# Opening of an attention and mixture-of-experts kernel: shift rows sent by SyncE, router constants made earlier or by ScalarE, one pair's copies held back

## The chip, the cores and the metric

The kernel runs on one core of a Trainium2 chip. Its engines are named as in the profile: PE is TensorE (PEld its weight loads), DVE is VectorE, ACT is ScalarE, POOL is GpSimd, SP is SyncE, which here only issues DMAs. A row marked SPq or ACTq is the issue of a DMA by that engine's sequencer. The metric is the device time of one execution in microseconds (us), as the median over runs.

## What is computed

Causal attention with a forgetting bias over 8 batches, 8 heads, 576 positions and head size 64, and then a two-level mixture of 16 experts on the 4608 resulting tokens. Cut to what matters:

```python
scores = q @ k.T / 8
cum = cumsum(maximum(s, 0))                    # per head
scores += minimum(-(cum[:, None] - cum[None, :]), 0);  scores[causal] = -1e9
attn = exp(scores - max(scores)) ;  x = (attn / sum(attn)) @ v
group = argmax(x @ w_group) ;  expert = argmax(x @ w_expert[group])
out = weight * (maximum(x @ w1[expert], 0) @ w2[expert])
```

## The kernel before, in words

Heads are handled in 32 pairs; pair p holds heads 2p and 2p+1. The loop `for step in range(-LEAD, NH + 5)` does at step n the scores and exponentials of head n, the product with the values of head n-1, and the row maxima of head n+4. The order of the work within a step is written out by hand in lists of letters (`FIRST`, `ORDERS`), so that the order on PE, DVE, ACT and POOL is fixed. Steps -4 to -1 do only the row maxima of the first four heads.

The operands of the scores stand in tiles that are used in turn. `WA` (four of them, `NA`) holds keys and queries rounded to fp32r, and below them the rows with the running sums (two) and the row shifts (two). `WB` (five, `NBB`) holds the low parts of the same. For each pair:

- `load_raw` (L159, SP) brings keys and queries, 576 KB, into a tile `r`; there are three.
- `split` (L166 on ACT, L170 on POOL, for the first pair on DVE) rounds them into `hl` and takes the low part. For the first four pairs `place` (L182, ACT) writes half of `WA` and `WB` directly.
- `load_a` (L191, L193, SP) copies `hl` and the sums into `WA`, and `load_b` (L203, L204, SP) copies `hl` into `WB`, from the fifth pair on in four copies of 144, 288, 144 and 288 KB. `load_v` (L207, SP) brings the values `VT`.
- `rowmax` (L228 on PE, L236 on DVE) gives the row maxima. When a pair has all of them, they are transposed (L250) and `shifts` (L256, L257 on DVE) makes their negative in two parts, `th` and `tl`, of 10 partitions by 128. `send` (L262) then issues two DMAs that write them as two rows of `WA`. In the kernel before, these DMAs are issued by ACT: 64 in all.
- `scores` (L284 and L286 on PE) needs these rows. It writes into a ring of three PSUM tiles `ps`, which come free when the exponential (L294, ACT) has read them. A head has five such units. `av` (L326) multiplies with the values into `po`, which come free when ACT has copied `vals` and `sums` (L331, L334).

Each DMA issued by SP or ACT ends on one of eight semaphores that are given out in turn over both queues (DMAHW0 to DMAHW7 in the listings below). The issue of a DMA waits until the DMA that used its semaphore before has landed. The issue also waits for the data it reads and for the place it writes. An engine's queue is in order, so whatever stands behind such an issue waits too.

The sums: `s` arrives, DVE scales and scans it (L530, L532), rounds it (L533) and subtracts (L534), and SP copies the two parts into the first `WA`. The router's constants (`ub`, `ob`, and through `ni` the two tables `part`) are made by DVE in `operands`, in between the row maxima of the third and fourth head.

## Time and profile before

| | us |
|---|---|
| three runs | 867.61, 872.62, 871.92; median 871.92 |
| the profiled execution | 869.25 |
| its span, first to last instruction | 867.4 |
| PE busy | 839.2 (97%) |
| DVE, ACT, POOL busy | 718.4, 615.0, 602.5 |

The attention takes somewhat less than the first half of the span; the experts follow. The page's 40 slices show PE at 90% or more busy in all but the first, the third and the last. A row of the timeline gives the start, the duration, the engine, the line, what is written from what, and in brackets the idle time of the engine ahead of it with what ended it. In a row of windows stand the window, its length, the busy time of each engine with the number of instructions, the granted clock of PE as a share of 2.4 GHz, the share of time the DMA engines were busy, and GB/s.

### The profile page before, as it was taken

How to read it: one execution, taken by the hardware profiler on the slowest of the kernel's cores; microseconds unless marked ns; L12 is line 12 of the kernel's file. 1: busy time of each engine (PE TensorE's matmuls, PEld its weight loads, DVE VectorE, ACT ScalarE, POOL GpSimd, SP SyncE). 2: the span in 40 equal slices, each digit the busy share in tenths (PEclk: the TensorE clock that was granted, in tenths of full speed). 3: DMA queues.
4: the chain of work that ended last, by engine and by line, in shares of the span. 5: the costliest groups of instructions: out<-in, count | busy, mean ns of one | idle time of the engine just before them, and what ended most of it. 6: DMA issues, size and time to landing. Idle time of an engine off the chain costs nothing. (4 is left out here: it accounts for less than half of the span.)

```text
span 867.4 us, 17805 instructions
## 1 busy us (share of the span) xinstructions
PE 839.2 (97%) x5601; PEld 771.9 (89%) x5601; DVE 718.4 (83%) x1982; ACT 615.0 (71%) x1393; POOL 602.5 (69%) x745
## 2 busy tenths in 40 slices
PE   4989999999999999999999999999999999999997
PEld 2778888888888888887789999999999999999996
DVE  7657788797878889787859799989999999999972
ACT  5668778786878778777747666776677777778760
POOL 9767677676876769545867756776677777777760
PEclk9999999999999999999999999999999999999999
DMA  7899898897979888633646645655566565666620
GB/s 197 266 233 250 234 235 232 213 248 194 248 209 245 236 221 225 177 87 122 194 149 225 245 151 208 205 164 193 201 201 216 188 216 195 223 228 214 215 96 26
DMA packets 82405, 174.06 MB, mean 201 GB/s; under 512 B 9692, under 2 KB 45660, under 8 KB 74112
## 3 DMA queue, kind: packets, MB, share of 16 engines
q1 hardware_dynamic: 72192, 153.20, 60.2%
q0 software_dynamic: 7488, 18.89, 5.7%
q10 hardware_dynamic: 2624, 0.76, 0.4%
q8 instruction: 46, 0.75, 0.3%
q14 instruction: 55, 0.45, 0.2%
HBM read 108.97 MB, written 19.69 MB: 148 GB/s over the span
## 5 line engine op out<-in xcount | busy, mean ns | idle before, releaser
L1067 POOL TENSOR_TENSOR wl<-raw,wh 128x512 fp32r<-128x512 f32 x163 | 209.8, 1299 | 82.5 <-ACT wh L1064 54.6
L236 DVE CUSTOM_DVE_ANT_0 mx<-pm,mask 128x192 bf16<-128x192 f32 (+4 forms) x320 | 127.3, 418 | 33.1 <-PE pm L228 30.4
L1064 ACT CAST wh<-raw 128x512 fp32r<-128x512 f32 x256 | 154.3, 616 | 0.0
L1189 PE MATMUL ph<-xh,wh 128*128 128x256 f32 (+13 forms) x512 | 140.2, 300 | 0.1
L1189 PE MATMUL ph<-xl,wh 128*128 128x256 f32 (+13 forms) x512 | 137.7, 300 | 0.1
L228 PE MATMUL pm<-WA 66*128 66x288 f32 (+4 forms) x384 | 123.8, 355 | 14.0 <-DMA WA<-ch 9.7
L284 PE MATMUL ps<-WA 68*128 68x320 f32 (+4 forms) x384 | 135.4, 356 | 1.7 <-DMA WA<-tl 1.6
L326 PE MATMUL po<-pt,VT 128*128 128x256 f32 (+3 forms) x512 | 119.0, 351 | 3.6 <-POOL pt L303 1.8
L1196 ACT ACTIVATE hh<-ph 128x256 fp32r<-128x256 f32 (+13 forms) x128 | 53.5, 418 | 85.5 <-PE ph L1189 83.3
L1269 PE MATMUL py<-hh,wh 128*128 128x256 f32 (+13 forms) x448 | 113.4, 302 | 0.1
L1269 PE MATMUL py<-hl,wh 128*128 128x256 f32 (+13 forms) x448 | 112.5, 301 | 0.0
L286 PE MATMUL ps<-WB 128*128 128x320 f32 (+4 forms) x384 | 110.2, 300 | 0.0
L1322 DVE STREAM_TRANSPOSE yr<-yT 32x384 f32<-32x384 f32 (+1 forms) x208 | 104.6, 503 | 4.5 <-ACT yT L1266 0.3
L326 PE MATMUL po<-pu,VT 128*128 128x320 f32 (+1 forms) x384 | 105.2, 382 | 0.0
L1159 DVE STREAM_TRANSPOSE xt<-xg 32x256 f32<-32x256 f32 (+1 forms) x208 | 102.3, 492 | 2.7
L326 PEld LDWEIGHTS po<-pt,VT 128*128 128x128 f32 x512 | 87.8, 191 | 16.6 <-POOL pt L303 2.5
L1189 PEld LDWEIGHTS ph<-xh,wh 128*128 128x128 f32 x512 | 95.3, 189 | 0.6 <-DVE hl L1197 0.3
L1189 PEld LDWEIGHTS ph<-xl,wh 128*128 128x128 f32 x512 | 94.7, 189 | 0.5 <-DVE xl L1142 0.3
L1189 PE MATMUL ph<-xh,wl 128*128 128x256 f32 (+13 forms) x512 | 91.9, 299 | 0.0
L170 POOL TENSOR_TENSOR WB<-r,hl 64x576 fp32r<-64x576 f32 x62 | 88.0, 1420 | 5.5 <-ACT hl L166 1.7
L228 PEld LDWEIGHTS pm<-WA 66*128 66x128 f32 (+1 forms) x384 | 68.9, 192 | 24.0 <-POOL WA L528 9.6
L422 POOL TENSOR_TENSOR xTl<-xT,xTh 128x512 fp32r<-128x512 f32 x29 | 37.0, 1275 | 75.9 <-ACT xTh L417 55.7
(255 smaller groups left out, 2001.0 us busy)
## 6 DMA issues: line engine op xcount, KB each, us to landing
raw<-in_w_dram SPq DMA_DIRECT2D x64, 1024.0 KB
r<-in_qk_dram SPq DMA_DIRECT2D x32, 576.0 KB
WA<-hl SPq DMA_DIRECT2D x60, 288.0 KB
WB<-hl SPq DMA_DIRECT2D x60, 288.0 KB
VT<-in_v_dram SPq DMA_DIRECT2D x32, 384.0 KB
WB<-hl SPq DMA_DIRECT2D x64, 144.0 KB
xs<-xr SPq DMA_DIRECT2D x15, 512.0 KB
WA<-cumd SPq DMA_DIRECT2D x56, 4.5 KB
```

What stands on the lines that cost most here:

```text
L170: (nc.vector if p < 1 else nc.gpsimd).tensor_tensor(out=hl[:, 2] if part else WB[p % NBB][0:64, KA, h], in0=r[hr, part], in1=hl[hr, part]. ...
L228: nc.tensor.matmul(ps[:rows, :cw], WA[i][0:66, QA, h, QO + q0:QO + q0 + rows], WA[i][0:66, KA, h, QO + c0:QO + c0 + cw], start=True, stop= ...
L236: nc.vector.tensor_tensor_reduce(out=tmp[:rows, :cw], in0=ps[:rows, :cw], in1=mk[:rows], scale=1.0, scalar=-3.0e38 if c0 == 0 else mo, op0 ...
L284: nc.tensor.matmul(ps[:rows, o:o + w], WA[i][0:68, KA, h, QO + k0:QO + k0 + rows], WA[i][0:68, QA, h, QO + q0:QO + q0 + w], start=True, st ...
L286: nc.tensor.matmul(ps[:rows, o:o + w], WB[p % NBB][:, KA, h, k0:k0 + rows], WB[p % NBB][:, QA, h, q0:q0 + w], start=False, stop=True)
L326: nc.tensor.matmul(po[0][:, qa - base:qb - base], VT[p % NVT].rearrange("p t a d -> p (t a d)")[:, (3 * t + 1 + h) * 64:][:, 0:P], x[:, c: ...
L1064: self.casts.append(nc.scalar.copy(h[:, j], raw[:, j]))
L1067: self.low = lows[self.u, i, j] = nc.gpsimd.tensor_tensor(out=l[:, j], in0=raw[:, j], in1=h[:, j].bitcast(F32), op=ALU.subtract)
L1159: V.transpose(dst[:, 0:n, :, j], src[:, 0:n, :, i])
L1189: self.product = nc.tensor.matmul(pss[f][:, :cap], w[f // 4][:, c, (f % 4) * P:(f % 4 + 1) * P], x[:, c, :cap], start=(c == 0 and w is sel ...
L1269: self.product = nc.tensor.matmul(pss[c][:, :cap], w[2 + f // 4][:, f % 4, c * P:(c + 1) * P], x[:, f, :cap], start=(f == 0 and w is self. ...
L1322: V.transpose(dst[:, 0:n, :, i], src[:, 0:n, :, j])
```

## The change

Four things are changed, all of them in the attention part.

1. `send` issues the DMAs of `th` and `tl` on SP's queue, for all 32 pairs.
2. The rounding of the sums (was L533) goes from DVE to ACT, and at the start `place(0, 0)` is put behind the first pair's `split`.
3. The router's constants: the four operations that make `part` stand ahead of the sums on DVE; `ub` and `ob` are written by ACT at the end of step -1; only the rounding of the router's weights stays among the row maxima, later than before.
4. The four `load_b` copies of the sixth pair (p = 5) are held until the last exponential of head 4, and behind the last `load_a` copy of their pair.

```diff
-                nc.sync.dma_start(w[64:66, KA, h, QO:].bitcast(F32), (cumh if p < 4 else cumd)[n:n + 1].bitcast(F32))
+                st.at["wa", p] = nc.sync.dma_start(w[64:66, KA, h, QO:].bitcast(F32), (cumh if p < 4 else cumd)[n:n + 1].bitcast(F32))
...
-                if h or not placed:
-                    nc.sync.dma_start(w[0:64, QA, h], hl[hr, 1])
-                nc.sync.dma_start(w[64:128, b, h], hl[hr, 0::2][:, b])
+                copies = [nc.sync.dma_start(w[0:64, QA, h], hl[hr, 1])] if h or not placed else []
+                copies.append(nc.sync.dma_start(w[64:128, b, h], hl[hr, 0::2][:, b]))
+                for i in copies if p == 5 else ():
+                    hold(tc, i, st.at["exp", 4])
+                    behind(tc, i, st.at["wa", p])
...
-                    nc.scalar.dma_start(WA[i][r:r + 1, QA].bitcast(F32).rearrange("o h q -> o (h q)"), t.bitcast(F32))
+                    nc.sync.dma_start(WA[i][r:r + 1, QA].bitcast(F32).rearrange("o h q -> o (h q)"), t.bitcast(F32))
...
+        nc.gpsimd.iota(n1, pattern=[[S, B], [P, NB]], base=1, channel_multiplier=1, allow_small_or_imprecise_dtypes=True)
+        for k, x, op in ((0, 6, ALU.arith_shift_right), (1, 63, ALU.bitwise_and)):
+            nc.vector.tensor_scalar(out=ni, in0=n1, scalar1=x, scalar2=None, op0=op)
+            nc.vector.tensor_copy(part[:, k], ni)
         nc.vector.tensor_scalar(out=r1, in0=s0, scalar1=0.0, scalar2=8.0, op0=ALU.max, op1=ALU.mult)
...
-        nc.vector.tensor_copy(cumh[:, 0], c2)
+        nc.scalar.copy(cumh[:, 0], c2)
...
-        place(0, 0)
         split(0, 0)
         split(0, 1)
+        place(0, 0)
         load_a(0, True)
...
                 nc.sync.dma_start(cumd, cumh.bitcast(F32))
+                nc.scalar.copy(rt.ub, rt.uf)
+                nc.scalar.copy(rt.ob, rt.onesf)
                 rt.queue.append(rt.operands())
...
-        yield 5
+        yield 11
         V.tensor_copy(self.wr_sb[:, :, 0:20], self.wr_f)
         V.tensor_tensor(out=self.wr_sb[:, :, 20:40], in0=self.wr_f, in1=self.wr_sb[:, :, 0:20].bitcast(F32),
                         op=ALU.subtract)
-        yield
-        V.tensor_copy(self.ub, self.uf)
-        yield
-        V.tensor_copy(self.ob, self.onesf)
-        yield
-        V.tensor_scalar(out=ni, in0=n1, scalar1=6, scalar2=None, op0=ALU.arith_shift_right)
-        V.tensor_copy(self.part[:, 0], ni)
-        yield
-        V.tensor_scalar(out=ni, in0=n1, scalar1=63, scalar2=None, op0=ALU.bitwise_and)
-        V.tensor_copy(self.part[:, 1], ni)
```

The order of PE's matmuls does not change in any row. What moves is seen in three places.

The first is SP's queue at the start, which in the kernel before reads as follows. `WA_107` and `WB_111` belong to the first pair, `WA_108` and `WB_112` to the second, `WA_109` with `r_135` and `hl_223` to the third; `r_346` holds the raw data of the fourth pair and `VT_116` the first values.

```order
L204 DMA WB_111<-hl_171 64x576
L193 DMA WA_109<-ch 2x1x576
L191 DMA WA_109<-hl_223 64x2x576
L193 DMA WA_109<-ch 2x1x576
L204 DMA WB_112<-hl_180 64x2x576
L203 DMA WB_112<-hl_180 64x576
L204 DMA WB_112<-hl_180 64x576
L207 DMA VT_116<-in_v_dram 128x6x128
L159 DMA r_346<-in_qk_dram 128x1152
```

In the changed kernel the same place of SP's queue reads as follows, with what each issue waits for; `hl_227` is the third pair's rounded data and `r_350` the fourth pair's raw data.

```order
L203 DMA WB_111<-hl_178 64x576 [waits DMAHW5_49]
L202 DMA WB_113<-hl_227 64x576 [waits DMAHW6_49,Activation_49]
L264 DMA WA_107<-th_293 1x10x128 [waits DMAHW7_49,DVE_49]
L264 DMA WA_107<-tl_294 1x10x128 [waits DMAHW0_49,DVE_49]
L193 DMA WA_109<-ch 2x1x576 [waits DMAHW1_49,Pool_49]
L191 DMA WA_109<-hl_227 64x2x576 [waits DMAHW2_49]
L193 DMA WA_109<-ch 2x1x576 [waits DMAHW3_49]
L203 DMA WB_112<-hl_188 64x2x576 [waits DMAHW4_49,Pool_49]
L202 DMA WB_112<-hl_188 64x576 [waits DMAHW5_49]
L203 DMA WB_112<-hl_188 64x576 [waits DMAHW6_49]
L209 DMA VT_116<-in_v_dram 128x6x128 [waits DMAHW7_49]
L159 DMA r_350<-in_qk_dram 128x1152 [waits DMAHW0_49]
```

Three issues have come in ahead of the third pair's first row of sums: a copy of the third pair's data, which waits for ACT, and the first pair's two shift rows. The raw data of the fourth pair are now the tenth issue behind the copy that waits for ACT.

The second place is ACT's queue at the fourth and fifth step of the loop (heads 4 and 5), before the change, with the waits. `th_711` and `tl_712` are the shift rows of the fourth pair.

```order
L294 ACTIVATE pt_118<-ps_2_0_692 128x512 [waits Pool_49]
L262 DMA WA_110<-th_711 1x10x128 [waits DMAHW4_49,DVE_49]
L262 DMA WA_110<-tl_712 1x10x128 [waits DMAHW6_49,DVE_49]
L334 ACTIVATE sums_596<-po_0_686 64x256
L294 ACTIVATE pu_119<-ps_0_256_702 128x320 [waits PE_49]
L294 ACTIVATE pt_118<-ps_4_0_719 64x64 [waits PE_49]
```

The two issues are gone from ACT's queue in the changed kernel:

```order
L296 ACTIVATE pt_118<-ps_2_0_692 128x512 [waits Pool_49]
L336 ACTIVATE sums_594<-po_0_686 64x256
L296 ACTIVATE pu_119<-ps_0_256_702 128x320 [waits PE_49]
L296 ACTIVATE pt_118<-ps_4_0_719 64x64 [waits PE_49]
L166 CAST hl_673<-r_591 128x576
```

The third place is SP's queue at the same time. Before, semaphore DMAHW6, for which the issue of `tl_712` above waits, was last used by the first copy into `WB_111`, which is the sixth pair's (`hl_580`).

```order
L207 DMA VT_116<-in_v_dram 128x6x128 [waits DMAHW4_49,PE_49]
L159 DMA r_743<-in_qk_dram 128x1152 [waits DMAHW5_49]
L203 DMA WB_111<-hl_580 64x576 [waits DMAHW6_49]
L191 DMA WA_108<-hl_580 64x2x576 [waits DMAHW7_49,PE_49]
L193 DMA WA_108<-cumd 2x576 [waits DMAHW0_49]
L204 DMA WB_111<-hl_580 64x2x576 [waits DMAHW1_49,Pool_49]
L203 DMA WB_111<-hl_580 64x576 [waits DMAHW2_49]
L204 DMA WB_111<-hl_580 64x2x576 [waits DMAHW3_49]
L159 DMA r_915<-in_qk_dram 128x1152 [waits DMAHW5_49]
```

In the changed kernel the four copies stand behind the next raw load and the shift rows, and the first of them waits for ACT; `hl_578` is the sixth pair's.

```order
L159 DMA r_743<-in_qk_dram 128x1152 [waits DMAHW5_49]
L191 DMA WA_108<-hl_578 64x2x576 [waits DMAHW6_49,PE_49]
L193 DMA WA_108<-cumd 2x576 [waits DMAHW7_49]
L159 DMA r_915<-in_qk_dram 128x1152 [waits DMAHW0_49,Pool_49]
L264 DMA WA_110<-th_711 1x10x128 [waits DMAHW1_49,DVE_49]
L264 DMA WA_110<-tl_712 1x10x128 [waits DMAHW2_49,DVE_49]
L193 DMA WA_109<-cumd 2x576 [waits DMAHW3_49,PE_49]
L202 DMA WB_111<-hl_578 64x576 [waits DMAHW4_49,Activation_49]
L191 DMA WA_109<-hl_673 64x2x576 [waits DMAHW5_49,Activation_49]
L203 DMA WB_111<-hl_578 64x2x576 [waits DMAHW6_49]
```

From there on, SP's queue has for nearly every pair the raw load, then `th` and `tl`, then the row of sums.

## Rows read from the trace of the kernel before

**Rows 1.** The page's first part: busy time, share and instructions of each engine.

```profile
PE 839.2 (97%) x5601; PEld 771.9 (89%) x5601; DVE 718.4 (83%) x1982; ACT 615.0 (71%) x1393; POOL 602.5 (69%) x745
```

**Rows 2.** Windows: three pairs of steps, and the stretch behind a stall.

```profile
34.43:47.86 13.43, 11.89 (x68) 9.21 (x66) 12.29 (x38) 9.97 (x23) 10.99 (x15) 1.00 0.91 240
47.86:62.38 14.52, 12.72 (x72) 11.09 (x70) 7.95 (x30) 9.36 (x23) 7.75 (x11) 0.88 0.94 232
62.38:73.30 10.92, 10.92 (x72) 9.75 (x70) 7.98 (x30) 8.77 (x24) 7.40 (x12) 1.00 0.89 229
55.30:58.70 3.40, 3.35 (x12) 3.08 (x13) 1.00 (x5) 2.76 (x7) 0.23 (x1) 0.50 0.86 250
```

**Rows 3.** Timeline, 44 to 55 us: the fourth pair's shift rows and SP's raw loads.

```profile
44.78 1.33 SPq L159 DMA_DIRECT2D r<-in_qk_dram  x1
...
50.44 0.28 DVE L257 SCALAR_TENSOR_TENSOR tl<-pmt,th 10x128 fp32r<-10x128 f32 x1
...
53.79 0.36 SPq L159 DMA_DIRECT2D r<-in_qk_dram  x1
54.10 0.73 ACTq L262 DMA_DIRECT2D WA<-tl  x1
...
54.87 0.38 ACT L334 ACTIVATE sums<-po 64x256 f32<-64x256 f32 x1 [3.53 <-DVE mc L236]
```

**Rows 4.** Timeline, 36 to 44 us: router constants on DVE, and ACT's exponential.

```profile
36.58 1.43 DVE L749 CAST ub<-uf 128x128 bf16<-128x128 f32 x1
...
40.26 0.54 ACT L294 ACTIVATE pu<-ps 128x448 f32<-128x448 f32 x1 [1.65 <-DVE mc L236]
...
43.42 0.18 DVE L757 CAST part<-ni 128x40 f32<-128x40 int32 x1
```

**Rows 5.** Timeline, 0 to 23 us: loads, casts and the first shift rows.

```profile
1.46 1.51 SPq L159 DMA_DIRECT2D r<-in_qk_dram  x3
...
4.17 0.50 DVE L530 TENSOR_SCALAR cl<-cl 64x576 f32<-64x576 f32 x1 [4.17 <-DMA cl<-in_s_dram]
...
5.65 1.15 ACT L182 CAST WA<-r 64x1152 fp32r<-64x1152 f32 x1 [3.03 <-DMA r<-in_qk_dram]
...
6.08 0.74 DVE L533 CAST ch<-cl 64x576 fp32r<-64x576 f32 x1
...
13.87 1.24 ACT L166 CAST hl<-r 128x576 fp32r<-128x576 f32 x2
...
18.07 0.74 ACTq L262 DMA_DIRECT2D WA<-tl  x1
...
18.67 0.61 SPq L207 DMA_DIRECT2D VT<-in_v_dram  x1
...
19.33 1.15 SPq L159 DMA_DIRECT2D r<-in_qk_dram  x2
...
22.21 0.55 PE L284 MATMUL ps<-WA 68*128 68x256 f32 x1 [1.57 <-DMA WA<-tl]
```

**Rows 6.** Timeline, 24 to 33 us: casts of the fourth pair, and PE's pace.

```profile
24.35 0.57 PE L286 MATMUL ps<-WB 128*128 128x448 f32 x1
...
26.81 1.15 ACT L182 CAST WA<-r 64x1152 fp32r<-64x1152 f32 x1
...
30.38 0.48 ACT L294 ACTIVATE pt<-ps 64x64 f32<-64x64 f32 x2
...
31.83 0.37 PE L286 MATMUL ps<-WB 128*128 128x448 f32 x1
...
32.19 0.31 PE L284 MATMUL ps<-WA 68*128 68x320 f32 x1
```

**Rows 7.** Timeline, 222 to 231 us: shift rows of a later pair, and its first scores.

```profile
222.23 0.75 SPq L159 DMA_DIRECT2D r<-in_qk_dram  x1
...
223.24 0.89 ACTq L262 DMA_DIRECT2D WA<-tl  x1
...
230.42 0.52 PE L284 MATMUL ps<-WA 68*128 68x256 f32 x1
```

More of the change, by code (lines that the diff above doesn't have):

```diff
@@ L528, in ones @@
                 nc.gpsimd.memset(WA[i][64:66 if a == QA else 68, a].bitcast(F32).rearrange("p h q -> p (h q)"), 1.0)
+        n1, ni = (ac.tile([P, B, NB], I32, name=n) for n in ("n1", "ni"))
+        part = ac.tile([P, 2, B, NB], F32, name="part")
+        nc.gpsimd.iota(n1, pattern=[[S, B], [P, NB]], base=1, channel_multiplier=1, allow_small_or_imprecise_dtypes=True)
+        for k, x, op in ((0, 6, ALU.arith_shift_right), (1, 63, ALU.bitwise_and)):
+            nc.vector.tensor_scalar(out=ni, in0=n1, scalar1=x, scalar2=None, op0=op)
+            nc.vector.tensor_copy(part[:, k], ni)
         nc.vector.tensor_scalar(out=r1, in0=s0, scalar1=0.0, scalar2=8.0, op0=ALU.max, op1=ALU.mult)
         nc.vector.tensor_tensor_scan(out=c2, data0=r1, data1=r1, initial=0.0, op0=ALU.add, op1=ALU.max)
-        nc.vector.tensor_copy(cumh[:, 0], c2)
+        nc.scalar.copy(cumh[:, 0], c2)
         nc.vector.tensor_tensor(out=cumh[:, 1], in0=c2, in1=cumh[:, 0].bitcast(F32), op=ALU.subtract)
@@ L562, in attention @@
         load_b(0, True)
-        rt = Router(tc, ac, late, end, small, ring, wr_f, wr_sb, xs, st)
+        rt = Router(tc, ac, late, end, small, ring, wr_f, wr_sb, part, xs, st)
         place(1, 1)
@@ L695, with __init__ @@
 class Router:
-    def __init__(self, tc, ac, sm, end, ps_t, ps_s, wr_f, wr_sb, xs, st):
+    def __init__(self, tc, ac, sm, end, ps_t, ps_s, wr_f, wr_sb, part, xs, st):
         self.end = end
@@ L732, in __init__ @@
         nc.gpsimd.iota(st.ie, pattern=[[1, E]], base=0, channel_multiplier=0, allow_small_or_imprecise_dtypes=True)
-        n1 = iota("n1", [[S, B], [P, NB]], base=1, cm=1, dt=I32)
-        self.part = ac.tile([P, 2, B, NB], F32, name="part")
-        ni = ac.tile([P, B, NB], I32, name="ni")
-        self.n1, self.ni, self.uf, self.onesf = n1, ni, uf, onesf
+        self.part, self.uf, self.onesf = part, uf, onesf
     def operands(self):
-        V, ni, n1 = self.tc.nc.vector, self.ni, self.n1
+        V = self.tc.nc.vector
         G = self.tc.nc.gpsimd
```

## The prediction

> **What bounds the kernel now.** The page's first part is read first: PE is busy 97% of the span [rows 1]. The change leaves PE's instructions and their order alone, so it can only win back time in which PE waits, or in which its clock is at the lower of its two levels (1.2 and 2.4 GHz). Second come windows that are cut at the same place of each pair, the first scores of its first head. A pair takes 10.92 us where PE is never idle; the fourth pair begins 14.52 us after the third, with PE idle for 14.52 - 12.72 = 1.80 of them and the clock at 0.88, and the third 13.43 us after the second [rows 2]. So 3.60 us are lost in the third pair's steps (4 and 5) and 2.51 us in the second pair's (2 and 3). Third, the opening in the timeline: PE waits 1.57 us for `tl` ahead of the first scores at 22.21 [rows 5]. A unit of 448 columns takes 0.57 us at 24.35 and 0.37 at 31.83 [rows 6]. So PE runs at the lower level until about 31, though the granted clock's column shows 1.00 there; a microsecond won ahead of that is not all won later. Everything later in the kernel has the same work on PE, and what the change touches there is SP's and ACT's queues alone.
>
> **The stall of steps 4 and 5: 3.6 us gained.** DVE has made `tl` by 50.72, yet ACT issues it at 54.10, and the `sums` behind it come at 54.87 after 3.53 us of idle time [rows 3]. The issue waits on a semaphore that the sixth pair's first `WB` copy holds (DMAHW6 in the order's rows). `po` stays full until `sums` is read, PE stands, and its clock falls: the next 3.40 us are granted 0.50 [rows 2]. With the two issues gone from ACT, `sums` waits only for PE. SP stands in this wait instead, but PE needs those two rows only at the next pair's scores, at 62.38 before and 58.8 after, and the 864 KB of the sixth pair are out of the way. I take the whole 3.60. Bounds: 1.8, if PE merely keeps its clock but waits for something else in that stretch, and 3.60.
>
> **The constants: 2.0 us gained.** `ub` alone keeps DVE 1.43 us at 36.58, ahead of the third pair's `th`; ACT then issues that pair's shift rows late and starts its exponential at 40.26 after 1.65 us of idle time [rows 4]. Both causes leave. What stays of the 2.51 us is ACT's part: casts of the next raw data that stand ahead of exponentials as before. The router's weights are rounded two operations later in the run, of no more than `ub`'s 1.43 us each. I take 2.0; bounds 1.0 and 2.51.
>
> The four moved operations cost 0.18 us (`part`) to 1.43 us (`ub`) each [rows 4], so 0.7 to 5.7 us in all, at the start, where DVE has nothing until the sums' input arrives at 4.17 [rows 5]. POOL makes their own input among its first instructions. They are hidden at 0.7, and at 5.7 delay the sums by 1.5 or more; `part` is one of them, so zero. ScalarE's rounding is half of the cast of 64x1152, 1.15 us, so 0.58; DVE's took 0.74 [rows 5]. Zero, give or take 0.3 for two changes of engine. `ub` and `ob` on ACT lie between its casts and its first exponential, which has to wait for the scores of 22.21. Zero.
>
> **The opening: 0.9 us lost.** Two things oppose each other. The first pair's shift rows now wait, on SP, behind a copy that needs ACT's last cast of the third pair. That cast ends at 13.87 + 1.24 = 15.11 before. ACT now starts when the scan has ended, at 6.08 instead of 5.65, with 0.6 of rounding ahead, so the cast ends at 16.2. Issues follow each other every 0.66 us (18.67 to 19.33 [rows 5]): `tl` goes at 17.5 instead of 18.07. It landed within 4.1 us before; the scores can then start between 20.6, when the row maxima are done, and 21.6. That gains 0.6 to 1.57. But the fourth pair's raw load is the tenth issue behind that copy: 16.2 + 10 x 0.68 = 23.0 instead of 19.33. A load takes between 4.2 us (the first one) and 7.5 (19.33 to 26.81, when ACT used it without a wait shown) [rows 5, 6], so it lands between 27.2 and 30.5; I take 28.2, near the first, as few copies stand ahead. ACT's casts of it take 30.38 - 26.81 = 3.57 us and stand ahead of the exponential of the second head's first 256 columns, which ends at about 32.1. That head's unit of 320 and 192 columns takes the place in the ring that this frees, and it started at 32.19 before [rows 6]. So PE arrives there 1.6 us earlier and waits for as long: nothing is gained, and PE has an idle stretch of 1.6 us just when its clock rose before. After the 1.80 us of the later stall it was granted 0.50 for 3.4 us [rows 2], which costs 1.7 us. I take half of that, 0.9 us lost. Bounds: 1.6 gained if the load lands by 27.2 and the clock rises, 3.5 lost if it lands at 30.5 and the clock stays down.
>
> **The queue of SP: nothing, then 0.5 us lost.** Each pair adds two issues of 0.72 to 0.89 us to SP [rows 7], 1.6 us of 10.92; behind them in the queue stand copies for later pairs. In [rows 7] the raw load's issue ends at 222.98, `tl` would be issued at 223.7 instead of 223.24, and the pair's scores are at 230.42, so landing may take 6.7 us. Zero. Without the stall the DMA engines, busy 0.89 to 0.94 in these stretches [rows 2], must bring the same bytes in less time, with the sixth pair's copies now close ahead of the fifth pair's shift rows. A landing of up to 9.0 us is seen where they are that busy (the raw load of 44.78, for which the one at 53.79 waits [rows 3]), against 8.1 from the rows' making to their use (50.72 to 58.8). I take 0.5 us, bounds 0 and 2.
>
> ScalarE's queue is also 64 issues of about 0.72 us lighter, but PE does not wait for it there. Zero.
>
> **A rule against the change.** The fact first: shift rows on ACT's queue never made PE wait after the first pair, with 6.3 us (224.13 to 230.42 [rows 7]) to land. The Trainium skill, "DMA: Bandwidth & Descriptors", section "Queues, rings and completion order", says that SP and ACT own a ring each on every DMA engine and that an engine serves the rings by turns, packet by packet. By that rule a small copy on ACT's own ring passes SP's backlog, and on SP's ring it goes behind the raw load issued just ahead of it; that is the third rival below. Its section "Issuing engines are not separate DMA queues" would make the move cost only issue time. No row here decides between them, as the span shows no landing time apart from waits.
>
> **The sum.** 3.6 + 2.0 - 0.9 - 0.5 = 4.2 us gained: 869.25 - 4.2 = 865.05 for an execution like the profiled one (span about 863.2, and 1.8 around it). The profiled one is 2.67 below the runs' median and 1.1 below the mean of all four, 870.35. I add 0.95 and say **866.0**.
>
> **Rivals.**
> First: the opening's gain stays too. The raw load lands by 27.2, so the ring does not block, and the clock rises as before. For it: the first load took 4.2 us. Against: ten issues, and busy DMA engines. Sum: 3.6 + 2.3 + 1.6 = 7.5, about 862.
>
> Second: the change does not do what it says. The stall is made by the DMA engines' backlog, so it moves: SP waits on the semaphore, the fourth or fifth pair's shift rows come late, and PE waits there instead. With the opening's clock lost as well: 1.8 + 2.0 - 2.6 - 1.0 = 0.2, about 870. For it: the DMA share is 0.94 over the stalled pair [rows 2]. Against: the rows have 8.1 us of room.
>
> Third, slower: SP's queue in order, and its ring, bring the shift rows after the raw load for every pair. The point from which it decides is a landing time of 6.7 us [rows 7]. At 7.1, PE waits 0.4 us in some 30 pairs, 12 us: about 878. At the 9.0 seen once [rows 3] it would be 2.3 us a pair, 69 us: about 935. Against: bytes and engines are the same as before, and 6.3 us sufficed in every pair.
>
> **Chances.** The forecast 0.54, the first rival 0.19, the second 0.18, the third 0.09. The range 860.5 to 873 takes in the first two rivals and the bounds of the opening (1.6 gained to 3.5 lost), and leaves out the third and tails of the rest, about 0.18. About 1% of 872, 8.7 us, is what a measurement of this kernel can tell from no change: faster means below 863.2, which takes half of the first rival and little of the forecast, 0.14; slower means above 880.6, part of the third rival, 0.05; the rest is 0.81.
>
> **What would show it.** In the changed profile the pair from step 4 should take 10.9 to 11.5 us and no window behind the opening should be granted 0.50. The second pair's should take 11 to 12. ACT should start the fourth pair's casts at about 28.2 (26.81 before), and PE should show a wait for ACT at a unit of 320 columns near 32. PE's waits for `tl` should not exceed 0.5 us after the first pair. I am wrong if the raw load lands early, if PE's low clock lasts beyond 38, or if `WA<-tl` appears among PE's waits for many pairs.

## The result, and the profile after

The changed kernel takes 874.31 us in the median of 8 runs (869.33 to 877.73), the kernel before 869.83 (867.61 to 872.62). The ratio is 1.0063, with a 95% interval of 1.0038 to 1.0087: half a per cent slower where half a per cent faster was forecast. The profiled execution took 871.60 us (span 869.8), 2.35 more than the one of before (869.25).

First the windows, cut as before at the first scores of each pair's first head. Columns: window, length, busy time of PE, PEld, DVE, ACT and POOL with instructions, the clock's column, DMA share, GB/s. The share comes out above 1.00 in places; that is read here as full engines.

```profile
20.68:37.42 16.74, 15.31 (x52) 12.59 (x52) 6.90 (x31) 8.19 (x17) 11.28 (x18) 1.00 0.97 271
37.42:49.71 12.29, 11.80 (x67) 10.02 (x66) 6.95 (x32) 10.06 (x23) 9.64 (x12) 1.00 0.95 224
49.71:60.65 10.94, 10.94 (x72) 9.77 (x70) 7.96 (x30) 8.75 (x23) 7.91 (x13) 1.00 1.01 260
60.65:73.28 12.63, 11.56 (x72) 9.73 (x70) 7.98 (x30) 10.01 (x25) 9.27 (x15) 1.00 1.00 242
73.28:85.04 11.76, 11.15 (x70) 9.66 (x70) 7.98 (x30) 9.26 (x23) 7.99 (x12) 1.00 1.07 266
```

The same windows of before that [rows 2] does not have:

```profile
22.21:34.43 12.22, 12.05 (x51) 10.57 (x52) 5.40 (x25) 8.07 (x17) 9.59 (x17) 1.00 0.91 289
73.30:84.21 10.91, 10.91 (x71) 9.74 (x70) 7.98 (x30) 9.14 (x24) 8.11 (x13) 1.00 0.95 272
```

The third pair, which took 14.52 us with the stall [rows 2], takes 10.94: the stall of steps 4 and 5 is gone, and so is the window at 0.50 behind it. The second gains 13.43 - 12.29 = 1.14. But the first pair takes 16.74 instead of 12.22, the fourth 12.63 instead of 10.92 and the fifth 11.76 instead of 10.91. At the sixth pair's first scores the change stands 85.04 - 84.21 = 0.83 us *behind*. PE's waits after (what PE ran, what it waited for: total us, times, longest) name the places:

```profile
PE ps L286 <- DMA WA<-tl: 1.6, 2, 1.0
PE pvr L1376 <- DVE xlr L1350: 1.3, 1, 1.3
PE ps L286 <- ACT pt L296: 1.1, 1, 1.1
PE ph L1186 <- DVE yr L1380: 1.1, 1, 1.1
```

The first row is two pairs' first scores that wait for their shift rows, the third the opening. The other two lie at the start of the experts, at 468.1 and 474.5 us; they are the rest of the 2.35 us (about 1.5), and the same is seen in kernels without the change (last section).

The opening, in the timeline (start, duration, engine, line, operation, idle time before it):

```profile
16.52 0.46 SPq L202 DMA_DIRECT2D WB<-hl  x1
17.07 0.84 SPq L264 DMA_DIRECT2D WA<-th  x1
18.02 0.77 SPq L264 DMA_DIRECT2D WA<-tl  x1
...
23.81 1.17 SPq L159 DMA_DIRECT2D r<-in_qk_dram  x2
```

```profile
28.94 1.15 ACT L182 CAST WA<-r 64x1152 fp32r<-64x1152 f32 x1 [2.70 <-DMA r<-in_qk_dram]
...
31.34 0.47 PE L230 MATMUL pm<-WA 66*128 66x320 f32 x1
32.95 0.63 PE L286 MATMUL ps<-WA 68*128 68x320 f32 x1 [1.15 <-ACT pt L296]
...
39.01 0.47 PE L288 MATMUL ps<-WB 128*128 128x320 f32 x1
...
41.64 0.32 PE L288 MATMUL ps<-WB 128*128 128x320 f32 x1
```

The fourth pair's raw load goes at 23.81 (19.33 before [rows 5]), ACT's casts of it start at 28.94, and PE waits 1.15 us at the unit of 320 columns, as forecast. What the prediction had only as a bound is the pace: a unit of 320 columns still takes 0.47 us at 39.01 and 0.32 only at 41.64, where before the full pace is there by 31.83 [rows 6]. PE runs eight microseconds longer at the lower of its two levels. The clock's column shows 1.00 here, as it did before; but 0.47 us is also what a unit of 320 columns takes in e14 at 78.96, in a stretch granted 0.50.

### The profile page after: what moved, and what is told of

Same layout as the page of the kernel before. It is cut to its first block, busy times and chain, and to the rows that moved or that the text cites. A ratio compares the mean times of both kernels' runs of the same rounds, so it can differ in the third digit from the quotient of the medians.

```text
span 869.8 us, 17850 instructions
## 1 busy us (share of the span) xinstructions
PE 840.8 (97%) x5601; PEld 773.1 (89%) x5601; DVE 718.5 (83%) x1979; ACT 616.7 (71%) x1396; POOL 601.2 (69%) x745
```

## The experiments

The theories are these. **A**: the loss is the opening; SP's in-order queue sends the fourth pair's raw load late. **B**: it is the shift rows that land late on SP. **C**: it is the experts' start. Two more came after the first four runs, to say why the gain does not stay even with the opening mended. **D**: the DMA engines are behind with their bytes, and a row waits for what was issued ahead of it. **E**: SP's own queue is the bound, since it now issues for more of the time. Each run is compared with runs of the kernel before on the same chip. The chips differ, so medians of different rows are not compared; the ratio is taken over all runs of both kernels and is not the quotient of two medians:

| kernel | median us | ratio to before, 95% |
|---|---|---|
| the change | 874.31 | 1.0063 (1.0038 to 1.0087) |
| e1 all rows back on ACT | 870.96 | 1.0011 (0.9996 to 1.0026) |
| e2 rows on SP, nothing else | 870.81 | 1.0026 (1.0005 to 1.0046) |
| e3 first two pairs' rows on ACT | 869.34 | 1.0012 (0.9994 to 1.0030) |
| e4 raw load sooner | 874.12 | 1.0047 (1.0022 to 1.0072) |
| e5 rows before raw loads | 872.90 | 1.0048 (1.0030 to 1.0066) |
| e6 e3, copies left out | 865.54 | 0.9961 (0.9948 to 0.9974) |
| e7 the change, no hold | 871.91 | 1.0036 (1.0019 to 1.0054) |
| e8 constants only | 869.85 | 1.0009 (0.9995 to 1.0023) |
| e9 e3, values early | 870.80 | 1.0008 (0.9985 to 1.0030) |
| e10 before, values early | 869.62 | 0.9996 (0.9967 to 1.0024) |
| e11 the change, values early | 875.14 | 1.0060 (1.0036 to 1.0083) |
| e12 before, copies left out | 867.22 | 0.9963 (0.9941 to 0.9984) |
| e13 e3, thin copies | 865.30 | 0.9944 (0.9924 to 0.9964) |
| e14 e3, one issue fewer a pair | 870.95 | 1.0015 (0.9997 to 1.0034) |
| e15 before, thin copies | 866.78 | 0.9966 (0.9951 to 0.9980) |
| e17 e3, sums on ACT's queue | 873.38 | 1.0048 (1.0023 to 1.0072) |
| v1, v2 ACT makes copies | 874.00, 873.26 | 1.0044 (1.0015 to 1.0072), 1.0043 (1.0021 to 1.0064) |

**The opening: e1 to e4.** e1 is the change with `send` on ACT again:

```diff
-                    nc.sync.dma_start(WA[i][r:r + 1, QA].bitcast(F32).rearrange("o h q -> o (h q)"), t.bitcast(F32))
+                    nc.scalar.dma_start(WA[i][r:r + 1, QA].bitcast(F32).rearrange("o h q -> o (h q)"), t.bitcast(F32))
```

e2 is the reverse of it, on the kernel before. In e3 the same line, in the change, begins with `(nc.scalar if p < 2 else nc.sync).dma_start(`.

> The change with its first part undone: the shift rows of all pairs go back to ScalarE's queue; constants, the rounding by ScalarE and the held copies of the sixth pair stay. Theory A (the loss is the opening: on SyncE's in-order queue the third pair's WB copy and the first shift rows stand ahead of the fourth pair's raw load, which went at 23.81 us instead of 19.33; ScalarE's casts come late and TensorE's clock rises at 39.5 instead of 31.4): the raw load's issue is back near 19 to 20, the clock is full by about 32, and the kernel gains 3 to 5 us on the change, about 869 to 871; if the held copies also free the wait at step 5, it falls to about 866. Theory B (shift rows on SyncE's queue land late: 1.6 us of waits at the fourth and fifth pairs): only 1.6 us come back, about 872.5, and the clock still rises at 39. Theory C (the loss is 3 us at the start of the experts and has nothing to do with queues): no gain, about 874.

> The kernel before with the first part alone: shift rows on SyncE's queue, nothing else. Theory A: the raw load goes at 23 to 24 us and the clock rises late as in the change; the stall of steps 4 and 5 (3.6 us) is gone, the constants' 2 us are not: about 874 to 877, that is 4 to 7 us slower than before. Theory B: as before less the stall plus 1.6 us of waits, about 868. Theory C: about 866 to 868, since the stall goes and nothing is lost in the opening.

> The change, but the first two pairs' shift rows go by ScalarE's queue and only the others by SyncE's: SyncE's rows up to the fourth pair's raw load then stand as in the kernel before. Theory A: raw load at about 19 to 20 us, clock full by about 32, no wait for ScalarE at the ring near 32; the stall of steps 4 and 5 stays away; 4 to 5 us faster than the change, about 866 to 870. Theory B: the waits for the fourth and fifth pairs' rows stay, and so does the loss: about 874. Theory C: about 874.

e2, with nothing but the rows moved, has the change's opening: the raw load at 23.18, the first pair 16.36 us, and 0.47 us for 320 columns at 38.42. In e1 and e3 the raw load goes at 20.74 and 20.73, 320 columns take 0.32 and 0.31 at 31.96 and 32.79, and the first pair takes 12.12 and 12.97. e3 differs from the change in the first two pairs' rows alone and takes back 1.0063 - 1.0012 = 0.5%, 4.4 us. So most of what the change *lost* lies in the order of the opening (theory A). Theory C is not quite out: of the 4.44 us between the two profiled executions about 1.5 are the experts' start, which is slow in the change's and not in e3's (last section). e2 came at 870.81, where A forecast 874 to 877 and B 868: no theory called it.

But neither is faster than before, though in e1 the rows are where they were and the constants and the held copies stay. Its windows show where the gain went:

```profile
34.06:46.08 12.02, 11.11 (x67) 9.15 (x66) 7.20 (x32) 10.07 (x23) 10.65 (x16) 1.00 0.93 239
46.08:57.02 10.94, 10.94 (x72) 9.77 (x70) 7.96 (x30) 8.75 (x23) 7.92 (x13) 1.00 1.01 262
57.02:73.94 16.92, 14.09 (x72) 12.42 (x70) 7.95 (x30) 9.93 (x24) 9.35 (x15) 0.80 1.02 248
```

```profile
63.47 0.72 ACTq L264 DMA_DIRECT2D WA<-th  x1
64.28 0.73 ACTq L264 DMA_DIRECT2D WA<-tl  x1
65.06 0.38 ACT L336 ACTIVATE sums<-po 64x256 f32<-64x256 f32 x1 [4.56 <-DMA WA<-th]
```

Second and third pair gain 5 us, and the fourth loses 6: the very wait of [rows 3] (ACT stands at the issue of a shift row, `sums` behind it, then PE, then the clock) is back one pair later. The held copies alone only move it. With the rows off ACT's queue and nothing held (e2) the third pair takes 10.91.

e4 writes the raw load ahead of the six copies that stood before it:

```diff
-        pre = {-2: [(load_a, 2, True)],
-               -1: [(load_b, 1, True), (load_v, 0), (load_raw, 3), (load_raw, 4)],
+        pre = {-2: [(load_raw, 3), (load_a, 2, True)],
+               -1: [(load_b, 1, True), (load_v, 0), (load_raw, 4)],
```

> The change, with the fourth pair's raw load written ahead of the third pair's six WA copies and the second pair's WB copies; all shift rows stay on SyncE's queue, so the load still stands behind the third pair's WB copy and the first shift rows. It should go at about 18.7 us instead of 23.8 and land near 24 to 25. Theory A, with the raw load as the cause: clock full near 32, no ring wait, about 869 to 871; the copies it overtakes go 0.7 us later and must not make the third pair's row maxima late by more than that. If it is the copies' lateness rather than the load's that keeps the clock down, the time stays at about 874. Theories B and C: about 874.

The load goes at 18.83 and 448 columns take 0.38 us at 33.20, so the full pace is back with the load. That the late load is what keeps the clock down is not shown, though: e7 below has the load at 23.80 and the full pace from 31.28. Of the four profiles with the load behind 23 us (the change, e2, e7, e11) three have the late clock, of the other sixteen none. The time is not back in e4: the overtaken copies make PE wait 2.2 us for `WA<-ch`, and the fourth pair takes 14.78 us with 2.6 us of wait for `tl`.

**Who takes the gain back: e3, e5, e6.** e3 has no late clock and no stall, and still:

```profile
57.83:69.03 11.20, 11.20 (x72) 9.75 (x70) 7.98 (x30) 9.45 (x24) 8.38 (x13) 1.00 0.92 214
69.03:81.98 12.95, 11.16 (x71) 9.67 (x70) 7.99 (x30) 9.84 (x25) 9.05 (x15) 1.00 1.02 264
```

Of its 2.8 us of waits for `tl` one (1.0) is the first pair's; the other, 1.8, ends the fifth pair. At the fourth pair's first scores this execution is 62.38 - 57.83 = 4.55 us ahead of the one of before, at the sixth's 84.21 - 81.98 = 2.23, and it ends 2.0 ahead. So the rows take half of the gain; why the median shows nothing of the other half cannot be read from this trace. e5 puts raw loads behind the rows (first diff, in `load_raw`); e6 leaves the WB copies of four pairs out (second, in `load_b`):

```diff
+            if 6 <= p <= 12:
+                behind(tc, st.at["raw", p], st.at["rows", p - 4])
```

```diff
-            for h in range(2):
+            for h in range(2) if not 5 <= p <= 8 else ():
```

> As the run in which the first two pairs' shift rows stay with ScalarE, and the raw loads of the seventh to the thirteenth pair are written behind the shift rows that stood just behind them on SyncE's queue. Every byte moves as before. Theory D (the DMA engines are behind with their bytes until about 85 us, and what goes through SyncE's queue is served in order, so that a row waits for all that was issued ahead of it): each such row has 576 KB less ahead of it, lands about 2 us sooner, the two waits of TensorE for the rows (2.8 us in all) go, and the time is about 865 to 867. If the backlog is paid in any case, the casts of the raw data or the WA copies come late in place of the rows, and the time stays at about 869.

> As the run in which the first two pairs' shift rows stay with ScalarE, with the 864 KB of WB copies of each of the sixth to the ninth pair left out (their scores then use what older pairs left in these tiles). All instructions of TensorE, VectorE and ScalarE stay. Theory D: the DMA share falls well below 0.9 between 45 and 90 us, all shift rows land at least 1 us ahead of their use, no TensorE wait for them and no half clock behind the opening: 863 to 866. If the rows are late for another reason (SyncE's issue time, waits for buffers), the waits of 1 to 2 us at the fifth and sixth pairs stay and so does the time, 868 to 870.

e5 failed: it is slower than e3. The waits for the fifth and sixth pair's rows are gone, but PE waits 1.2 us for values at 53.64 and 0.8 for ACT at 74.08, and at 134.63, where nothing waited before, 2.8 for `tl`, with a fall of the clock behind it. The DMA engines fell to a share of 0.91 between 50 and 60 us (0.97 in e3) and were at 1.01 from 60 to 90: what was held back seems to have been missing later. e6 is the fastest so far, with no wait for rows behind the opening, and its 5 runs lie within 0.8 us.

**The parts by themselves: e7, e8.** e7 drops the hold from the change (first diff); e8 is the kernel before with the change's constants alone (second).

```diff
-                for i in copies if p == 5 else ():
+                for i in ():
```

```diff
+            nc.vector.tensor_scalar(out=ni, in0=n1, scalar1=x, scalar2=None, op0=op)
+            nc.vector.tensor_copy(part[:, k], ni)
...
+                nc.scalar.copy(rt.ub, rt.uf)
+                nc.scalar.copy(rt.ob, rt.onesf)
```

> The change without its last part: the sixth pair's WB copies are not held back. Theory D: the same bytes come a little sooner, nothing else waits on them, and the time is that of the change, 873 to 876. If the hold is what takes the stall of steps 4 and 5 away, the stall is back and it is 2 to 4 us slower; if the hold itself makes later rows late, it is 1 to 3 us faster.

> The kernel before with the third part alone: the router's constants made ahead of the sums or by ScalarE. The second pair should fall from 13.43 to about 12 us by the prediction's term. Theory D: what is won there is lost again at the stall of steps 4 and 5, which ends with the DMA traffic and not a fixed time behind the third pair's start: that pair grows from 14.52 to about 16, and the time stays at 868 to 870. If the stall goes along unchanged, the kernel gains 1.4 to 2 us: about 867.

In e7 the third pair takes 13.58 us instead of 10.94: PE waits 1.6 us for values there. Without the hold SP itself waits 1.8 us for a transfer at the issue of the next pair's rows, and `tl` goes out at 57.43. Its time is no worse than the change's, though (the intervals overlap), and in its profiled execution the full pace is there from 31.28, with the change's order of the opening:

```profile
31.28 0.31 PE L230 MATMUL pm<-WA 66*128 66x320 f32 x1
```

The same matmul takes 0.47 at 31.34 in the change. Both are ahead of the wait for ACT (1.28 us at 32.88 in e7, 1.15 at 32.95 in the change), so that wait is not what parts the two.

In e8 the second pair takes 12.02. The third takes 12.16, where theory D forecast about 16 and the kernel before takes 14.52: ACT stands there too, but PE waits 1.00 us instead of 1.80, and the clock does not fall.

```profile
47.91:60.07 12.16, 11.16 (x71) 9.73 (x70) 7.97 (x30) 8.45 (x21) 7.63 (x13) 1.00 1.06 288
```

```profile
54.61 0.67 PE L328 MATMUL po<-pt,VT 128*128 128x256 f32 x2 [1.00 <-issue]
```

The profiled execution is 1.5 us faster than before, and the median is not.

**Less on the DMA engines early: e9, e10, e11.** The first two loads of values go to stretches in which the engines have little to do:

```diff
             load_raw(p)
+        load_v(0)
...
         load_b(0, True)
+        load_v(1)
```

> As the run in which the first two pairs' shift rows stay with ScalarE, with the first two VT loads (384 KB each) moved to stretches in which the DMA engines have little to do: the first behind the three raw loads (share 0.04 from 8 to 10 us), the second behind the first pair's WB copies (share 0.15 from 16 to 18 us). The computation is whole. Theory D: about 3 us of DMA time leave the stretch from 20 to 36 us, everything behind lands 1.5 to 3 us sooner, TensorE's waits for the rows of the fifth and sixth pairs (2.8 us) fall below 1, and the time is 865 to 867, less than before. If the loads only get in the way of the first pair's WA copies, the first matmul comes up to 1.5 us later and the time is 870 to 872.

> The kernel before, with the first two VT loads moved in the same way and nothing else. Theory D: the stall of steps 4 and 5 (3.6 us) comes from ScalarE's queue waiting for a transfer, so it shrinks by the 1.5 to 3 us that the DMA engines win: 866 to 868. If that stall does not hang on the backlog, about 869.

> The change with the first two VT loads moved in the same way. Theory D: the waits of the fourth to sixth pairs (1.6 us) go, and with them the half clock that other executions have there; the late clock in the opening (about 4 us) stays or shrinks by 1 to 2 us: 867 to 871, 3 to 7 us faster than the change. Otherwise about 874.

All three missed: 1.0008, 0.9996 and 1.0060, as without the move. (In e10's profiled execution the third pair takes 12.17 us, as in e8.) In e9 the fifth and sixth pair's rows still come late, and the DMA share from 60 to 100 us is 1.05. So the load there is not carried over from the opening, as theory D had it.

**Bytes or issues: e12 to e17.** e6 had taken away transfers and their issues. e12 does the same to the kernel before. e13 and e15 (on the kernel before) keep each issue and cut the copies' columns with `e = 36 if 5 <= p <= 8 else S`:

```diff
-                copies = [nc.sync.dma_start(w[0:64, QA, h], hl[hr, 1])] if h or not placed else []
-                copies.append(nc.sync.dma_start(w[64:128, b, h], hl[hr, 0::2][:, b]))
+                copies = [nc.sync.dma_start(w[0:64, QA, h, :e], hl[hr, 1, :e])] if h or not placed else []
+                copies.append(nc.sync.dma_start(w[64:128, b, h, :e], hl[hr, 0::2][:, b, :e]))
```

e14 keeps the bytes and makes one issue of a pair's two for the sums; e17 puts both on ACT's queue with `(nc.sync if p < 4 else nc.scalar)`:

```diff
+                elif h:
+                    st.at["wa", p] = nc.sync.dma_start(w[64:66, KA, :, QO:].bitcast(F32),
+                                                       cumd[2 * p:2 * p + 2].rearrange("h a s -> a h s"))
```

> The kernel before, with the 864 KB of WB copies of each of the sixth to the ninth pair left out (their scores use what older pairs left in these tiles), and nothing else. Theory D: the stall of steps 4 and 5 goes without any change of queue, since the transfer for which ScalarE's issue waits is among those left out or is done sooner: about 865 to 867, within 1.5 us of the changed queues with the same copies left out (865.5). If the stall needs the rows off ScalarE's queue to go, about 868.5, and the change's first part is worth its 3 us where the DMA engines have room.

> As the run in which the first two pairs' shift rows stay with ScalarE, with the WB copies of the sixth to the ninth pair cut to 36 of their 576 columns (the rest of the tile keeps what older pairs left): SyncE issues as many transfers as before, but 94% of these copies' bytes are gone. Theory D (the bytes on the DMA engines make the rows late): as where the copies were left out, 865 to 866.5, and no wait for rows at the fifth and sixth pairs. Theory E (SyncE's queue itself is the bound: 45 issues between 45 and 85 us keep it busy for 32.7 of 40 us, against 36 and 22.2 in the kernel before, and a row waits for its turn there): the issues stay, so the waits of 1 to 2 us stay, 868 to 870.

> The kernel before with the WB copies of the sixth to the ninth pair cut to 36 of their 576 columns, every issue staying. Theory D: as the kernel before without these copies (0.9963 of before), 866 to 867. If what helped there was the issues left out and not the bytes, the stall of steps 4 and 5 stays and the time is 869.

> As the run in which the first two pairs' shift rows stay with ScalarE, with the two transfers of a pair's sums (WA<-cumd, 2x576 each) made one from the fifth pair on: one issue fewer in each pair on SyncE, the same bytes, the same result. Theory D: nothing changes, 868 to 870. Theory E: some 0.6 us of SyncE's time come free in each pair, rows go earlier by as much, and about half of the 2.8 us of waits go: 867 to 868.

> As the run in which the first two pairs' shift rows stay with ScalarE, with the transfers of the sums (WA<-cumd) on ScalarE's queue from the fifth pair on: two issues fewer in each pair on SyncE, as many as the shift rows added, and the same bytes. Theory D: the rows land as late as with the sums on SyncE; and ScalarE stands again where such an issue waits for a transfer: 869 to 872. Theory E: SyncE's queue is as light as in the kernel before, the waits for rows go, 866 to 867.

Most of it goes with the bytes and not with the number of issues. The window from 60 to 90 us, of e13, e15, e3, e17 and the kernel before, in this order:

```profile
60.00:90.00 30.00, 30.00 (x195) 26.75 (x195) 22.83 (x85) 24.81 (x63) 21.69 (x32) 1.00 0.71 186
```

```profile
60.00:90.00 30.00, 30.00 (x190) 26.77 (x189) 21.88 (x83) 25.04 (x63) 22.40 (x33) 1.00 0.64 168
```

```profile
60.00:90.00 30.00, 28.21 (x178) 24.74 (x177) 21.30 (x79) 22.83 (x56) 19.83 (x29) 1.00 1.00 241
```

```profile
60.00:90.00 30.00, 26.70 (x164) 22.64 (x163) 19.90 (x72) 22.50 (x56) 18.74 (x28) 1.00 1.07 241
```

```profile
60.00:90.00 30.00, 30.00 (x191) 26.57 (x189) 21.74 (x82) 24.80 (x64) 23.49 (x36) 1.00 0.91 239
```

Where the copies are thin, PE never waits in these 30 us and the share is 0.64 to 0.71. With whole copies and SP relieved of as many issues as the rows added (e17), PE is idle for 3.3 us at a share of 1.07: 1.9 of them for rows and 1.0 for an exponential of ACT, which now issues the sums. As a test of the issues this is weak: an issue of sums takes 0.4 us and one of a row 0.8, so e17 gives SP back half of the time that the rows cost it and e14 a quarter; and thin copies are also issued faster (two in 1.41 us in e13 at 60.06, in 1.69 in e3 at 59.86). The kernel before does not wait here either, at 0.91: it can be said to have paid already, in the stall of step 5, in which the engines went on at 0.86 [rows 2]. One row's way shows how: in e17 `tl` of the fifth pair is made by 61.80 and SP issues it at 66.26; in e13 it is made by 60.92 and issued at 63.14.

```profile
61.52 0.28 DVE L259 SCALAR_TENSOR_TENSOR tl<-pmt,th 10x128 fp32r<-10x128 f32 x1
```

```profile
66.26 0.76 SPq L264 DMA_DIRECT2D WA<-tl  x1
```

So E is right in part: the row does wait in SP's queue, 4.5 us. In e17 a copy ahead of it stands 2.0 us for a transfer to land (issued at 58.56); in the change itself SP issues without a pause from 59.84 to 68.57, and the row waits for its turn. Taking these few issues off SP does not shorten the wait; taking bytes off the engines does, to 2.2. The thin copies also give what the change is worth where the engines have room. e15's pairs are 13.42 and 11.40 us from the second pair on, e13's 12.03 and 10.93:

```profile
35.51:48.93 13.42, 11.89 (x67) 9.19 (x66) 12.28 (x38) 9.98 (x23) 10.64 (x14) 1.00 0.92 241
48.93:60.33 11.40, 11.15 (x71) 9.73 (x70) 7.97 (x30) 8.45 (x21) 6.72 (x10) 1.00 0.73 196
```

```profile
35.10:47.13 12.03, 11.11 (x68) 9.15 (x66) 7.20 (x32) 10.09 (x23) 10.74 (x17) 1.00 0.90 232
47.13:58.06 10.93, 10.93 (x72) 9.76 (x70) 7.96 (x30) 8.75 (x23) 7.90 (x13) 1.00 0.83 220
```

That is 1.39 us for the constants and 0.47 for the rows, 1.86 in all, and the ratios differ by 0.9966 - 0.9944 = 0.22%, 1.9 us; their intervals overlap, and the medians, taken on one chip, differ by 1.48. The other such pair, e6 and e12, differs by 0.02% alone. So with room on the engines the change is worth between nothing and two microseconds, and the kernel before gains as much from fewer bytes without any change of queue.

**A version with the whole computation: v1, v2.** ACT makes the fifth (and sixth) pair's first copies from the raw data, as it does for the first four:

```diff
-               1: [(split, 4, 0), (split, 4, 1), (load_b, 2, True), (load_raw, 5)]}
+               1: [(split, 4, 0), (split, 4, 1), (load_b, 2, True), (load_raw, 5), (place, 4, 0)],
+               2: [(place, 4, 1), (place, 4, 2)],
+               3: [(place, 5, 0)], 4: [(place, 5, 1), (place, 5, 2)]}
```

The last line is v2's alone.

> As the run in which the first two pairs' shift rows stay with ScalarE, and three copies of the fifth pair's first and second head (WA 64x2x576, WB 64x576 twice) are made by ScalarE straight from the raw data, as it already makes them for the first four pairs: 576 KB less on the DMA engines before 55 us, 2.4 us more on ScalarE (casts of 0.62 to 1.15 us). The result is whole. Theory D: the DMA engines are 2.3 us less behind when the fifth and sixth pairs' rows go out, so most of TensorE's 2.8 us of waits go: 866 to 868, faster than before. If ScalarE's casts make exponentials late instead, 869 to 871.

> The same for the fifth and the sixth pair: 1152 KB less on the DMA engines before 70 us, 4.8 us more on ScalarE, which is busy for 0.7 to 0.9 of that stretch. The result is whole. Theory D: no waits for rows remain, no half clock behind the opening, 865.5 to 867, and the runs lie within 2 us of each other as where the bytes were left out. If ScalarE becomes the bound there, 869 to 872.

Both missed. In v2 the DMA share falls to 0.39 between 50 and 60 us and is 1.05 again from 60 to 90, with waits for rows as in e3; and the casts make an exponential late, so PE waits at a unit and its clock falls (0.51 from 47.20 to 50.60):

```profile
45.98 0.42 PE L286 MATMUL ps<-WA 68*128 68x320 f32 x1 [1.54 <-ACT pu L296]
```

No kernel that computes everything beats the one before in its median.

## Why the prediction was wrong

The sum, term by term, for the profiled execution:

| term | forecast | measured | from |
|---|---|---|---|
| stall of steps 4 and 5 | +3.6 | +3.58 | 14.52 - 10.94 |
| constants | +2.0 | +1.14 | 13.43 - 12.29 |
| opening | -0.9 | -2.99 | first scores 22.21 - 20.68, first pair 12.22 - 16.74 |
| SP's queue | -0.5 | -2.56 | 10.92 - 12.63, 10.91 - 11.76 |
| experts' start | none | -1.52 | 2.35 - 0.83 |
| sum | +4.2 | -2.35 | |

**The stall** went as said, to 0.02 us. The error was to count it as time lost for nothing: in it the DMA engines, at 0.94 [rows 2], brought what the later pairs need, and where it is gone and the bytes are not, PE waits for rows two pairs on (e3 against e13). A second doubt is about its size. About half of the 3.6 us is the fall of the clock, and e8 and e10, with the rows on ACT's queue as before, stall there without it: 12.16 and 12.17 us instead of 14.52. One execution of the kernel before was traced; if others go as e8's and e10's, part of the 3.6 us was never in its median. No run here decides that.

**SP's queue** is the step that failed: "`tl` would be issued at 223.7 instead of 223.24", 0.5 us late and so nothing. For that pair it holds: `tl` is made by 223.22 and issued at 223.85. But the row was taken from a calm place. In the fifth pair, where the engines are full, `tl` is made by 63.51 and goes out at 67.79, 4.3 us later, and PE waits for it until 73.28:

```profile
63.23 0.28 DVE L259 SCALAR_TENSOR_TENSOR tl<-pmt,th 10x128 fp32r<-10x128 f32 x1
```

```profile
61.17 1.74 SPq L202 DMA_DIRECT2D WB<-hl  x2
63.00 0.82 SPq L191 DMA_DIRECT2D WA<-hl  x1
63.87 0.44 SPq L193 DMA_DIRECT2D WA<-cumd  x1
64.41 1.69 SPq L203 DMA_DIRECT2D WB<-hl  x2
66.14 0.63 SPq L159 DMA_DIRECT2D r<-in_qk_dram  x1
66.88 0.81 SPq L264 DMA_DIRECT2D WA<-th  x1
67.79 0.78 SPq L264 DMA_DIRECT2D WA<-tl  x1
```

```profile
73.28 0.36 PE L286 MATMUL ps<-WA 68*128 68x256 f32 x1 [0.96 <-DMA WA<-tl]
```

Of the 8.1 us of room that the prediction gave a row, the queue alone takes half, and the landing takes 5.4 more (issued at 67.79, landed at 73.14 by the trace's semaphore updates). Of the 2.56 us in the table 1.6 are PE's waits for the two rows; the rest is mostly PE's busy time, 11.56 and 11.15 us instead of 10.92 and 10.91. The second rival (the stall moves, PE waits for the fourth or fifth pair's rows, about 870, chance 0.18) is the nearest to what came; the third, late rows in every pair, came in two pairs only.

**The opening** is the term that was mis-sized. The times in it all stood: `tl` at 18.02 (17.5 forecast), scores at 20.68 (20.6 to 21.6), the raw load at 23.81 (23.0), casts from 28.94 (28.2), the wait at the unit of 320 columns 1.15 (1.6). Only the clock's price was taken from the wrong row: half of what a fall to 0.50 costs in the middle of the kernel, 0.9 us, where here the rise came 8 us later. PE's busy time in the first pair grew from 12.05 to 15.31, so the pace alone cost 3.26 us, idle time 1.26, against 1.53 won at the start. It lies inside the bound of 3.5 that the prediction gave. The prediction's reason, an idle stretch of PE at the moment at which the clock rose before, is not borne out: in the change the pace is low ahead of that stretch, and in e7 it is full ahead of the same stretch.

**The constants** gave 1.14 and not 2.0 because the first 2 us of the second pair still ran at the lower pace; at the full pace the pair takes 12.02 in e1 and e8, a gain of 1.41. What stays of the 2.51 is not ACT's casts, as was said: PE's longest wait there, 0.76 us at 41.01 in e1, is for POOL's masking of `pt`, which stands behind POOL's part of the `split` (begun after a wait of 0.96 us for ACT's cast). The moved operations were not free: the four take 1.23, 1.11, 0.60 and 0.36 us ahead of the sums (`part` took 0.18 in the middle of the kernel [rows 4]), so the sums' first operation starts at 4.50 instead of 4.17 [rows 5] and the first matmul 0.34 us later than before. That is 3.3 us in all, between the ends of 0.7 and 5.7. ScalarE's rounding costs nothing that shows: e8, with DVE's, starts its first matmul as late.

```profile
1.37 1.23 DVE L536 TENSOR_SCALAR ni<-n 128x40 int32<-128x40 int32 x1 [1.37 <-POOL n L534]
2.63 1.11 DVE L537 CAST part<-ni 128x40 f32<-128x40 int32 x1
...
4.50 0.56 DVE L538 TENSOR_SCALAR cl<-cl 64x576 f32<-64x576 f32 x1
```

**The step from one execution to the median** went the wrong way: 0.95 us was added, and the median is 2.71 above the profiled run. The other runs' mean granted clocks are 0.991 to 0.998, against 0.999. In e1, e4 and e14 the profile caught such an execution: the clock falls to 0.50 for 3.4 to 6.8 us behind a wait in the fourth pair or at the fifth's first scores. In e14, with the wait in front:

```profile
74.48 0.55 PE L290 MATMUL ps<-WA 68*128 68x256 f32 x1 [2.87 <-DMA WA<-tl]
```

```profile
74.50:81.30 6.80, 6.80 (x24) 6.13 (x24) 2.58 (x9) 3.13 (x7) 3.71 (x5) 0.50 1.07 260
```

So a wait of 2.6 to 2.9 us can cost 1.7 to 3.4 more (half of the time at 0.50); behind e3's wait of 1.79 the clock does not fall. Where the bytes are gone (e13) six runs lie within 0.74 us. That the change's own longer runs lost their time there was not seen in a trace of them.

On the rule weighed in the prediction: by the trace's semaphore updates `tl` of the third to the seventh pair lands 3.5 to 6.1 us after its issue in the kernel before and 4.2 to 7.2 in e1, both on ACT's queue, and 4.8 to 6.3 in the change, on SP's. So a row on ACT's queue shows no sign of passing SP's backlog, and the third rival's mechanism is not seen; what a row loses on SP it loses mostly ahead of its issue. e3 and e17 have different transfers on SP's and ACT's queues, and the engines are as full in both (1.00 and 1.07 from 60 to 90 us). The Trainium skill, "DMA: Bandwidth & Descriptors", section "Issuing engines are not separate DMA queues", says that the transfers of all issuers run on the same engines, so that another issuer saves issue time alone; the traces agree as far as they go, with these shares and landings.

What stays open: which transfers make the stretch from 60 to 90 us heavier than the later ones, since less traffic before 60 (e9, v2) does not help; why the clock rises at 31 us in e7 and at 39 in the change with the same order of the opening; and in which executions of the kernel before the clock falls in step 5.

## What to carry to other kernels

Before a stall is counted as lost time, look at what else ran in it: where the DMA engines are at 0.9 or more, they used it, and the next transfer that is needed may be late instead; cutting the bytes of some copies, issues kept, shows what a reordering could be worth at most. Price a move of issues onto an in-order queue at the place where that queue is held up most, not in a calm pair, and follow it through the first iterations by themselves. A fall of the clock seen in one execution is not yet part of the median: look at a second one.

## What was not expected of the hardware

The 1.5 us at the experts' start have a cause of their own. VectorE's small instruction `idl<-lists` takes 0.27 us in the kernel before and 3.25 after; first the kernel before, then the change, then the change's POOL:

```profile
460.99 0.27 DVE L674 SCALAR_TENSOR_TENSOR idl<-lists 128x64 f32<-128x64 f32 x1
```

```profile
460.38 3.25 DVE L684 SCALAR_TENSOR_TENSOR idl<-lists 128x64 f32<-128x64 f32 x1
```

```profile
457.24 6.26 POOL L1064 TENSOR_TENSOR wl<-raw,wh 128x512 fp32r<-128x512 f32 x5
```

It ends at 463.63, 0.13 us behind POOL's run of five products (463.50). Before, POOL stood still from 460.17 to 461.34, and the instruction fell into that gap. Seven of the twenty profiled executions show the long form (the change, e9 to e12, v1, v2), e10 and e12 with the queues of before among them, so the change does not make it; it goes with where POOL's run falls. From the experts' first matmul to the end the seven take 1.5 to 1.6 us more than the kernel before, the other twelve at most 0.7. The Trainium skill, "GPSIMD Engine Reference", section "1. Specifications", says that GpSimd shares its SBUF interfaces with VectorE and that instructions with two SBUF inputs contend; this one has two, and the trace agrees, though here the instruction lasted until POOL's run of several had ended.
